# Regrouping the short TensorE work of an attention unit: transposes into slot 1, everything else into slot 4

## The chip, the cores and the metric

The kernel runs on one core of a Trainium2 chip. The metric is device time in microseconds for one execution; the median of several runs counts. A profile is one more execution, taken with the hardware profiler.

The engines are named as in the profile: PE is TensorE (PEld its weight loads), ACT is ScalarE, DVE is VectorE, POOL is GpSimd, SP is SyncE. SPq, PEq and so on are their instruction queues.

## The reference

Attention with RMS-normalized queries and keys, then a mixture of experts in which each token goes to one expert. All is float32.

```
q_n, k_n = rmsnorm(q, g_q), rmsnorm(k, g_k)          # q, k, v: (8, 12, 448, 64)
scores = q_n @ k_n^T / sqrt(64)
attn = exp(scores - max(scores)); attn /= sum(attn) + 1e-9
x = (attn @ v), heads side by side                   # 3584 tokens x 768
logits = x @ w_gate + modality_bias[modality_id]     # 8 experts
e = argmax(logits); gate = softmax(logits)[e]
out[token] = gate * (relu(x @ w1[e]) @ w2[e])        # w1: 768 x 1024, w2: 1024 x 768
```

## The kernel before

The first half of the span is attention, the second the experts; the change is in the first. Attention works in 48 **units** (u = 0 to 47), each a pair of heads of one batch row (12 heads make 6 units to a row, 8 rows). A unit has seven **slots** (j = 0 to 6); slot n = 7u + j is one turn of the loop at line 1172. In each slot TensorE first computes one tile of the transposed scores, `st` (line 848): two matmuls, four in slot 3, whose exp ScalarE writes as the tile `p`. Then it computes one tile `sa` (line 816), a rough score of the unit two ahead, of which VectorE takes the row maxima. These matmuls read operands of the type float32r. Both `st` and `sa` have two PSUM buffers.

All other TensorE work is short and is put into slots by due times:

- `tr` (line 742): four transposes of the normalized keys (g = 1) or queries (g = 0) of the unit three ahead. It returns four parts: `a0`, a ScalarE copy and two moves by DMA; `dve`, a VectorE subtraction for the low part and two more moves; `a1` and `a2`, casts on ScalarE (for queries each with a small one more).
- `mt` (line 835): transposes the seven columns of row maxima; ScalarE copies the result, and a DMA (line 843, on SyncE's queue from u = 2 on) puts it into row 64 of `ql`. There the second `st` matmul of the unit's slot 0 reads it, since the maximum is subtracted inside the matmul.
- `av` (line 887): the product of `p` with the values, four of them to a unit (c = 0 to 3), each for two heads, in plain float32: two instructions a head. After c = 3 `avcopy` takes the sum out.
- `sums` (line 904): eight matmuls every second unit, column sums of `p`. `gates` (line 913) and `recips` (line 925): once in four units. `xt` (line 946): four transposes of the output of a unit; its VectorE part writes `x`, and every third one stores it (line 967).

**What sets the order.** The dictionary `PLAN` (line 34) holds due times: `av`, `xt`, `sm`, `la`, `rc` are slots after the start of the following units for av, xt, sums, gates and recips (lines 1145 to 1170); `mt`, `tk`, `tq` are slots ahead of a unit's own start for mt and the two transposes; `first` holds single exceptions by unit. From u = 36 on, gates and recips are held to 4 and 6 at most and sums take `sml`, which is 4. Within a slot the loop writes instructions in the order of its lines, and each engine runs them in that order. `at(pre["A"], n + 1, f)` puts `f` on ScalarE ahead of the exp of the next slot, `pre["V"]` on VectorE ahead of the maximum, and `post` behind both in the slot named. The DMAs of these parts go into SyncE's queue in the same order, together with the loads of queries and keys (line 675), four loads of values (lines 666 and 668) and the x stores.

In slots of a steady unit u, the before has: slot 0 the key transposes (for u + 3), slot 1 two av (for u - 1) and mt (for u + 1), slot 2 sums and recips where due, slot 3 the query transposes, slot 4 one av and xt, slot 6 the last av and gates where due. `tr`, `mt`, `xt` and `recips` take turns on two PSUM buffers (tag "t").

Of the kernel before, what the change touches and what calls it, by code (L numbers as in the profile page):

```python
# [66 lines left out]
def kernel(  # L67
# [15 lines left out]
    V, A, G = (Deferred(e, n) for e, n in ((nc.vector, "op"), (nc.scalar, "act"), (nc.gpsimd, "dma")))  # L83
# [562 lines left out]
    if True:  # L646
# [31 lines left out]
        def sumsq(u, i):  # L678
# [156 lines left out]
        def mt(u):  # L835
            t = T[u]
            ps = ps_t.tile([128, 512], F32, tag="t", name=f"mt{u}")
            PE.transpose(ps[0:NJ, :128], t["mx"], idn)

            def act():  # L840
                ms = ms_b[u % 2]
                A.copy(ms, ps[0:NJ, :128])
                (A if u < 2 else SY).dma_start(t["ql"][64:65].rearrange("p h s -> p (h s)").bitcast(F32),
                            ms.bitcast(F32))

            return act
# [206 lines left out]
        P = PLAN  # L1053
# [6 lines left out]
        puts, done, routed = [], [], []  # L1060
# [71 lines left out]
        P = PLAN  # L1132
# [39 lines left out]
        for n in range(P["start"], NJ * NU):  # L1172
            i, j = divmod(n, NJ)
            todo = {}
            for what, *a in plan.get(n, ()):
                todo.setdefault(what, []).append(tuple(a))
            state["n"] = n
            state["rush"] = i >= P["rushat"]
            warm(P["warm"].get(n, 0))
            ex = st(i, j) if 0 <= i < NU else None  # L1180
            sm = [sa(*a) for a in todo.get("sa", ())]
            if n < 0:
                warm(P["warmn"])
            for u, c in todo.get("av", ()):
                av(u, c)
                if c == 3:
                    at(pre["A"] if j else post, n + (j > 0), lambda u=u: avcopy(u))
            for a in todo.get("sums", ()):
                sums(*a)
            for a in todo.get("gates", ()):  # L1190
                at(pre["A"], n + 1, gates(*a))
            for a in todo.get("tr", ()):
                a0, a1, a2, d_ = tr(*a)
                if a[0] < P["early"]:
                    at(pre["A"], n + 1, a1)
                    at(pre["A"], n + 1, a2)
                    at(pre["A"], n + P["late0"], a0)
                    at(pre["V"], n + P["late0"], d_)
                    continue
# [6 lines left out]
            for a in todo.get("recips", ()):
                at(pre["V"], n + 1, recips(*a))
                at(pre["V"], n + 1, lambda a=a: done.append(a[0]))
            for a in todo.get("xt", ()):
                at(pre["V"], n + 1, xt(*a))  # L1210
# [186 lines left out]
    nv = nc.values_load(state["nsl"], min_val=0, max_val=NS1 + NS2)  # L1397
# [52 lines left out]
```

## Time and profile before

| | |
|---|---|
| median of 3 runs | 1126.03 us (1123.86 to 1131.41) |
| the profiled execution | 1130.37 us, span 1128.6 us |
| TensorE busy | 1075.7 us, 95% of the span |
| VectorE, ScalarE, GpSimd busy | 858.9, 826.7, 659.0 us |
| mean granted TensorE clock | 0.978 |

In the views of the profile a row of the timeline is: start in us from the start of the span, duration, engine, line of the kernel, operation, output<-inputs by tile names, partitions x elements, and count; in brackets the time that the engine idled ahead of it and what it waited for. Tiles that share memory carry the name of the shared buffer: `w1w` holds the operands of st and sa, `xw` the high and low parts of the transposes and the copied maxima, `xrw` the normalized inputs, `at_hlw` among others the maxima, `r2w` and `at_w2lw` the exps and the values. L52 is the helper that records most ScalarE, VectorE and GpSimd work. In rows of groups the numbers after the bar are busy time, mean ns of one, and idle time ahead with its causes. Matmuls are pipelined and their ends are modelled: the difference of two starts is the safer measure.

### The profile page before, as it was taken

The numbers are of one execution on the slowest core, as the hardware profiler recorded it, in microseconds if no ns is written. First come the engines' busy times: TensorE is split into PE (matmuls) and PEld (weight loads), VectorE is DVE, ScalarE is ACT, GpSimd is POOL, SyncE is SP. The second block draws the span as 40 slices with busy tenths as digits, with TensorE's granted clock in tenths as the row PEclk, the third lists the DMA queues.
The fourth block names the chain that finished last, engine by engine and source line by source line (L and its number), as shares of the span: only waits on it lengthen the run. The fifth ranks groups of instructions, "written<-read, shape, count | busy, mean of one in ns | idle before, by whom it ended". The sixth has DMA issues, their size and how long they took to land.

```text
span 1128.6 us, 19979 instructions
## 1 busy us (share of the span) xinstructions
PE 1075.7 (95%) x6678; PEld 836.1 (74%) x6678; DVE 858.9 (76%) x1598; ACT 826.7 (73%) x1605; POOL 659.0 (58%) x665
## 2 busy tenths in 40 slices
PE   7899999999999999999999999999999999999993
PEld 6655555555455555554559899999999999999991
DVE  4577788988789788889698978767777677776770
ACT  6778888878788688876677677667876677766870
POOL 4478677779677697777864565354234433445340
PEclk8799999999999899999999999999999999999997
DMA  7656677667576777665824202111160111111360
GB/s 176 153 130 158 153 175 174 156 164 176 135 178 143 161 160 163 168 143 110 239 85 145 51 21 71 29 57 57 44 265 29 57 43 56 33 40 57 107 199 8
DMA packets 127970, 131.79 MB, mean 117 GB/s; under 512 B 68891, under 2 KB 122607, under 8 KB 126320
## 3 DMA queue, kind: packets, MB, share of 16 engines
q1 hardware_dynamic: 110212, 88.58, 33.9%
q0 software_dynamic: 17616, 41.80, 11.7%
q8 instruction: 57, 0.93, 0.4%
q14 instruction: 57, 0.47, 0.2%
q10 hardware_dynamic: 28, 0.01, 0.0%
HBM read 148.74 MB, written 22.38 MB: 152 GB/s over the span
## 4 chain that ended last, share of the span: by engine, by line
PE 74%; DVE 10%; DMA 7%; ACT 3%; issue 2%; SPq 1%; POOL 1%; ACTq 0%; DVEq 0%; POOLq 0%
PE ph L485 17%; PE py L515 16%; PE av L894 13%; PE st L855 12%; PE sa L827 4%; DMA lt<-l_d,tb_li 4%; PE tr L750 3%; DVE w1w L52 2%; DVE at_hlw L52 2%; PE xt L951 2%; DMA w1w<-xw 2%; PE sm L909 2%; PE px L468 2%; DVE xw L52 1%; DVE w2lw L52 1%
## 5 line engine op out<-in xcount | busy, mean ns | idle before, releaser
L485 PE MATMUL ph<-xw,w1w 128*128 128x256 f32 x2016 | 246.1, 283 | 3.1 <-DVE hlw L52 2.3
L485 PEld LDWEIGHTS ph<-xw,w1w 128*128 128x128 f32 x2016 | 243.9, 192 | 5.1 <-DVE hlw L52 2.5
L52 DVE TENSOR_REDUCE at_hlw<-sa 128x1 f32<-128x448 f32 x336 | 206.4, 617 | 49.5 <-PE sa L827 30.1
L52 DVE TENSOR_TENSOR w1w<-r,w1w 128x256 fp32r<-128x256 f32 x360 | 221.3, 674 | 13.3 <-ACT w1w L52 13.3
L52 ACT CAST w1w<-r 128x256 fp32r<-128x256 f32 x360 | 225.3, 726 | 0.0
L855 PE MATMUL st<-w1w 128*128 128x448 f32 (+1 forms) x480 | 177.3, 418 | 3.1 <-ACT r2w L52 3.0
L52 ACT ACTIVATE r2w<-st 128x448 f32<-128x448 f32 x168 | 91.1, 544 | 50.0 <-PE st L855 42.8
L52 ACT ACTIVATE hhw<-ph 128x512 fp32r<-128x512 f32 x56 | 33.5, 597 | 123.0 <-PE ph L485 123.0
L827 PE MATMUL sa<-w1w 128*128 128x448 f32 (+1 forms) x288 | 110.5, 384 | 9.8 <-DVE at_hlw L52 5.5
L855 PEld LDWEIGHTS st<-w1w 128*128 128x128 f32 (+1 forms) x480 | 85.7, 192 | 46.0 <-ACT r2w L52 23.7
L52 POOL TENSOR_TENSOR r2w<-r2w 128x448 f32<-128x448 f32 (+1 forms) x72 | 82.8, 1151 | 59.1 <-DVE r2w L52 18.3
L515 PE MATMUL py<-w2lw,hhw 128*128 128x384 f32 x448 | 113.9, 335 | 0.0
L52 ACT ACTIVATE at_w2lw<-st 128x448 f32<-128x448 f32 x168 | 91.0, 544 | 24.1 <-PE st L855 17.8
L855 PE MATMUL st<-w1w,w2ha 65*128 65x448 f32 x288 | 102.4, 376 | 5.3 <-DMA w1w<-xw 5.3
L52 ACT CAST w1w<-xw 64x448 fp32r<-64x448 f32 x188 | 105.3, 561 | 2.0
L52 POOL DMA_INDIRECT out_dram<-yw,lb_oi x22 | 26.7, 1215 | 123.5 <-ACT yw L52 120.5
L52 POOL TENSOR_TENSOR xrw<-r,at_hlw 112x512 f32<-112x512 f32 x95 | 97.4, 1044 | 1.0 <-PE tr L750 0.7
L515 PEld LDWEIGHTS py<-w2lw,hhw 128*128 128x128 f32 x448 | 80.8, 188 | 0.0
L52 DVE SCALAR_TENSOR_TENSOR hlw<-ph,hhw 128x512 fp32r<-128x512 f32 x56 | 38.6, 690 | 52.0 <-ACT hhw L52 51.9
L52 POOL TENSOR_TENSOR r2w<-r2w,at_w2lw 64x448 f32<-64x448 f32 (+1 forms) x48 | 55.6, 1157 | 32.3 <-DVE r2w L52 16.6
L52 ACT ACTIVATE xrw<-r 112x512 f32<-112x512 f32 (+1 forms) x124 | 64.7, 527 | 11.4 <-DMA r<-in_k_dram 8.1
L827 PEld LDWEIGHTS sa<-w1w 128*128 128x128 f32 (+1 forms) x288 | 55.6, 193 | 22.0 <-DVE at_hlw L52 9.7
(299 smaller groups left out, 2256.9 us busy)
## 6 DMA issues: line engine op xcount, KB each, us to landing
w1w<-xw SPq DMA_DIRECT2D x312, 112.0 KB
r<-in_q_dram SPq DMA_DIRECT2D x48, 224.0 KB
r<-in_k_dram SPq DMA_DIRECT2D x48, 224.0 KB
w2ha<-xw SPq DMA_DIRECT2D x72, 112.0 KB
x_d<-at_w2hb SPq DMA_DIRECT2D x8, 672.0 KB
x_d<-yw SPq DMA_DIRECT2D x8, 672.0 KB
r2w<-in_v_dram SPq DMA_DIRECT2D x48, 96.0 KB
at_w2lw<-in_v_dram SPq DMA_DIRECT2D x48, 96.0 KB
```

Source lines behind the costliest of these rows:

```text
L52: return fn(*a, **kw)
L468: PE.transpose(ps[:, i, 128 * t : 128 * t + 128], xr[t][:, 2 * g + i], idn)
L485: PE.matmul(ps[:, i], lhsT=lt_, rhs=rt_[:, c], start=n == 0, stop=n == 17)
L515: PE.matmul(ps[n][:, :384], lhsT=lt_[:, j, 128 * t : 128 * t + 128], rhs=rt_[:, 384 * n : 384 * n + 384], start=j == 0 and m == 0, stop=j ...
L750: PE.transpose(sp[:, c], src[:, c], idn[:CP, :CP])
L827: PE.matmul(ps[:, :S], lhsT=t["qq"][r, h, a : a + 128], rhs=t["kk"][h][r], start=True, stop=True)
L855: PE.matmul(ps[:, :S], lhsT=l, rhs=t["qq"][:, h] if first else t["ql"][:, h], start=first and (j != 3 or h == 0), stop=not first and (j != ...
L894: PE.matmul(t["av"][64 * h : 64 * h + 64, :S], lhsT=vv[r, u % 3, j], rhs=t["p"][r, j], start=c == 0, stop=c == 3)
L909: PE.matmul(R[g][32 * i : 32 * i + 32, :S], lhsT=sel[:, m], rhs=T[u + i // 2]["cs"][:, i % 2], start=m == 0, stop=False, tile_position=(0, ...
L951: PE.transpose(ps[:CP, 128 * c : 128 * c + 128], T[u]["xt"][:, c * CP : (c + 1) * CP], idn)
```

## The change

Two things change: numbers in `PLAN`, and the order in which the loop writes the short work of a slot. In `PLAN` (one line in the kernel, here only the entries that differ):

```diff
-'av': (1, 1, 4, 6), 'sm': 2, 'la': 6, 'rc': 9, 'mt': 6, 'tk': 21, 'tq': 18
+'av': (1, 1, 4, 4), 'sm': 4, 'la': 4, 'rc': 6, 'mt': 3, 'tk': 20, 'tq': 20
-'first': ('nq', 9): 31, ('nq', 8): 35, ('mt', 8): 50, ('mt', 5): 30, ('tk', 9): 43, ('mt', 6): 36, ('mt', 4): 22
+'first': ('nq', 9): 32, ('nq', 8): 29, ('tk', 3): 1, ('tk', 4): 8
```

In slots: key and query transposes both go to slot 1, the last av to slot 4 beside the third, mt to slot 4, sums and gates to slot 4, recips to slot 6. xt stays in slot 4 (in slots 2 and 5 for the last eight units, as before).

In the loop, `tr`, `mt`, `recips` and `xt` are now written ahead of `av`, `sums` and `gates`, and the parts of `tr` come sooner: `a0` and `dve` behind the exp and the maximum of the same slot, `a1` ahead of the next slot's exp and `a2` behind it.

```diff
             if n < 0:
                 warm(P["warmn"])
+            for a in todo.get("tr", ()):
+                a0, a1, a2, d_ = tr(*a)
+                if a[0] < P["early"]:
...
+                    continue
+                at(post, n, a0)
+                at(post, n, d_)
+                at(pre["A"], n + 1, a1)
+                at(post, n + 1, a2)
+            for a in todo.get("mt", ()):
+                at(pre["A"], n + 1, mt(*a))
+            for a in todo.get("recips", ()):
+                at(pre["V"], n + 1, recips(*a))
+                at(pre["V"], n + 1, lambda a=a: done.append(a[0]))
+            for a in todo.get("xt", ()):
+                at(pre["V"], n + 1, xt(*a))
             for u, c in todo.get("av", ()):
                 av(u, c)
...
             for a in todo.get("gates", ()):
                 at(pre["A"], n + 1, gates(*a))
-            for a in todo.get("tr", ()):
-                a0, a1, a2, d_ = tr(*a)
...
-                at(pre["A"], n + 1, a0)
-                at(pre["V"], n + 1, d_)
-                at(post, n + 1, a1)
-                at(pre["A"], n + 2, a2)
-            for a in todo.get("mt", ()):
-                at(pre["A"], n + 1, mt(*a))
...
```

The instructions themselves, their shapes and their number stay as they are.

More of the change, by code (lines that the diff above doesn't have):

```diff
@@ L33 @@
 ET = mybir.EngineType
-PLAN = {'rtj': 6, 'rushat': 36, 'av': (1, 1, 4, 6), 'xt': 4, 'xte': (2, 5), 'sm': 2, 'la': 6, 'rc': 9, 'csv': (1,), 'csj': (3, 6), 'csd': (1, 1), 'cse': (2, 1), 'sa': 14, 'mt': 6, 'tk': 21, 'tq': 18, 'nq': 26, 'nk': 26, 'sk': 49, 'sq': 50, 'rs': 48, 'ld': 58, 'first': {('sq', 0): -22, ('sk', 0): -22, ('nk', 0): -21, ('nq', 0): -20, ('sq', 1): -21, ('sk', 1): -21, ('sq', 2): -20, ('sk', 2): -20, ('nk', 1): -18, ('nq', 1): -18, ('tk', 0): -18, ('tq', 0): -18, ('sa', 0): -14, ('tk', 1): -13, ('tq', 1): -11, ('sa', 1): -7, ('mt', 0): -6, ('tk', 2): -8, ('tq', 2): -8, ('nq', 2): -14, ('nk', 2): -14, ('nq', 3): -2, ('nk', 3): -1, ('sq', 3): -8, ('sk', 3): -8, ('sq', 4): -9, ('sk', 4): -9, ('sq', 6): -6, ('sk', 6): -4, ('sk', 7): -7, ('sq', 8): 5, ('sk', 8): 5, ('nk', 7): 15, ('nq', 9): 31, ('tq', 3): 4, ('mt', 1): 0, ('nq', 5): 10, ('mt', 8): 50, ('rs', 0): -21, ('rs', 2): -18, ('nq', 8): 35, ('rs', 5): -7, ('mt', 2): 8, ('nq', 7): 18, ('mt', 5): 30, ('sk', 9): 15, ('tk', 9): 43, ('mt', 6): 36, ('nq', 6): 13, ('sa', 5): 22, ('rs', 7): 0, ('rs', 8): 6, ('mt', 4): 22, ('nk', 4): 4, ('ld', 9): 6, ('tk', 5): 15}, 'rs0': {0: 0, 2: 1, 5: 0, 7: 0, 8: 2}, 'sastep': 1, 'start': -22, 'warm': {5: 2, -6: 16, -12: 4, -7: 2, -9: 4, -21: 4}, 'warmn': 2, 'early': 1, 'late0': 1, 'pmp0': 2, 'ramp': 10, 'pmp': (0, 0, 1, 1, 1, 0, 1), 'nv': [(2, 1)], 'pmpa': (1, 0, 1, 0, 1, 1, 1), 'rush': (1, 1, 1), 'ps': [(7, 1)], 'pa': [(6, 0), (6, 1), (5, 1), (5, 0)], 'rtr': 6, 'sml': 4}
@@ new lines @@
+PLAN = {'rtj': 6, 'rushat': 36, 'av': (1, 1, 4, 4), 'xt': 4, 'xte': (2, 5), 'sm': 4, 'la': 4, 'rc': 6, 'csv': (1,), 'csj': (3, 6), 'csd': (1, 1), 'cse': (2, 1), 'sa': 14, 'mt': 3, 'tk': 20, 'tq': 20, 'nq': 26, 'nk': 26, 'sk': 49, 'sq': 50, 'rs': 48, 'ld': 58, 'first': {('sq', 0): -22, ('sk', 0): -22, ('nk', 0): -21, ('nq', 0): -20, ('sq', 1): -21, ('sk', 1): -21, ('sq', 2): -20, ('sk', 2): -20, ('nk', 1): -18, ('nq', 1): -18, ('tk', 0): -18, ('tq', 0): -18, ('sa', 0): -14, ('tk', 1): -13, ('tq', 1): -11, ('sa', 1): -7, ('mt', 0): -6, ('tk', 2): -8, ('tq', 2): -8, ('nq', 2): -14, ('nk', 2): -14, ('nq', 3): -2, ('nk', 3): -1, ('sq', 3): -8, ('sk', 3): -8, ('sq', 4): -9, ('sk', 4): -9, ('sq', 6): -6, ('sk', 6): -4, ('sk', 7): -7, ('sq', 8): 5, ('sk', 8): 5, ('nk', 7): 15, ('nq', 9): 32, ('tq', 3): 4, ('mt', 1): 0, ('nq', 5): 10, ('rs', 0): -21, ('rs', 2): -18, ('nq', 8): 29, ('rs', 5): -7, ('mt', 2): 8, ('nq', 7): 18, ('sk', 9): 15, ('nq', 6): 13, ('sa', 5): 22, ('rs', 7): 0, ('rs', 8): 6, ('nk', 4): 4, ('ld', 9): 6, ('tk', 5): 15, ('tk', 3): 1, ('tk', 4): 8}, 'rs0': {0: 0, 2: 1, 5: 0, 7: 0, 8: 2}, 'sastep': 1, 'start': -22, 'warm': {5: 2, -6: 16, -12: 4, -7: 2, -9: 4, -21: 4}, 'warmn': 2, 'early': 1, 'late0': 1, 'pmp0': 2, 'ramp': 10, 'pmp': (0, 0, 1, 1, 1, 0, 1), 'nv': [(2, 1)], 'pmpa': (1, 0, 1, 0, 1, 1, 1), 'rush': (1, 1, 1), 'ps': [(7, 1)], 'pa': [(6, 0), (6, 1), (5, 1), (5, 0)], 'rtr': 6, 'sml': 4}
@@ L1183 @@
                 warm(P["warmn"])
+            for a in todo.get("tr", ()):
+                a0, a1, a2, d_ = tr(*a)
+                if a[0] < P["early"]:
+                    at(pre["A"], n + 1, a1)
+                    at(pre["A"], n + 1, a2)
+                    at(pre["A"], n + P["late0"], a0)
+                    at(pre["V"], n + P["late0"], d_)
+                    continue
+                at(post, n, a0)
+                at(post, n, d_)
+                at(pre["A"], n + 1, a1)
+                at(post, n + 1, a2)
[6 more added lines that the diff above has]
+                at(pre["V"], n + 1, xt(*a))
             for u, c in todo.get("av", ()):
@@ L1191 @@
                 at(pre["A"], n + 1, gates(*a))
-            for a in todo.get("tr", ()):
-                a0, a1, a2, d_ = tr(*a)
[L1194 to L1199, printed above, removed]
-                at(pre["A"], n + 1, a0)
-                at(pre["V"], n + 1, d_)
-                at(post, n + 1, a1)
-                at(pre["A"], n + 2, a2)
-            for a in todo.get("mt", ()):
-                at(pre["A"], n + 1, mt(*a))
[L1206 to L1210, printed above, removed]
             if puts and n >= puts[0][0] and n - lastput[0] >= 3:
```

## The prediction

> **What bounds the kernel now.** I read the head of the page first, then TensorE's timeline through one unit, then SyncE's queue.
>
> ```profile
> span 1128.6 us, 19979 instructions
> PE 1075.7 (95%) x6678; PEld 836.1 (74%) x6678; DVE 858.9 (76%) x1598; ACT 826.7 (73%) x1605; POOL 659.0 (58%) x665
> ```
>
> TensorE is busy 95% of the time, but a busy TensorE is not TensorE at its peak, so what matters is when each matmul starts. Here is one attention unit without sums, and then the sums of the next unit (start, duration; "x4" counts instructions).
>
> ```profile
> 300.89 0.55 PE L750 MATMUL tr<-idn,xrw 112*128 112x112 f32 x4
> 301.21 0.66 PE L855 MATMUL st<-w1w 128*128 128x448 f32 x2
> 301.70 0.37 PE L827 MATMUL sa<-w1w 128*128 128x448 f32 x1
> 302.00 1.72 PE L894 MATMUL av<-r2w,at_w2lw 128*64 128x448 f32 x8
> 303.65 0.28 PE L838 MATMUL mt<-idn,at_hlw 128*7 128x128 f32 x1
> ...
> 305.21 0.37 PE L822 MATMUL sa<-xw,w2ha 128*128 128x448 f32 x1
> 305.41 0.55 PE L750 MATMUL tr<-idn,xrw 112*128 112x112 f32 x4
> ...
> 306.22 0.37 PE L827 MATMUL sa<-w1w 128*128 128x448 f32 x1
> 306.52 0.97 PE L894 MATMUL av<-r2w,at_w2lw 128*64 128x448 f32 x4
> 307.43 0.65 PE L951 MATMUL xt<-idn,at_hlw 128*112 128x128 f32 x4
> 307.83 0.66 PE L855 MATMUL st<-w1w 128*128 128x448 f32 x2
> 308.32 0.37 PE L827 MATMUL sa<-w1w 128*128 128x448 f32 x1
> 308.53 0.57 PE L855 MATMUL st<-w1w 128*128 128x448 f32 x2
> 308.94 0.37 PE L827 MATMUL sa<-w1w 128*128 128x448 f32 x1
> 309.24 0.97 PE L894 MATMUL av<-r2w,at_w2lw 64*64 64x448 f32 x4
> 310.14 0.47 PE L855 MATMUL st<-w1w 128*128 128x448 f32 x1
> ...
> 310.87 0.55 PE L750 MATMUL tr<-idn,xrw 112*128 112x112 f32 x4
> ...
> 314.15 0.36 PE L827 MATMUL sa<-w1w 128*128 128x448 f32 x1
> 314.45 0.57 PE L909 MATMUL sm<-at_w2lw,sel 128*32 128x448 f32 x2
> ...
> 315.33 0.68 PE L855 MATMUL st<-w1w 128*128 128x448 f32 x2
> ```
>
> From transpose to transpose the unit takes 310.87 - 300.89 = 9.98 us, with no idle time in any row: TensorE sets the pace here. Three things can be read off the starts. (a) Two st matmuls take 308.94 - 308.53 = 0.41 after an sa, but 0.49 after a short group (301.21 and 307.83 to the next sa): an **exit** costs 0.08. (b) From sa to the next st is 0.21 (308.32 to 308.53), from sa to av or sm 0.30 (301.70, 306.22, 314.15): an **entry** into these costs 0.09 more; into transposes none (305.21 to 305.41). (c) One value product takes 0.91 and 0.90 (306.52, 309.24 to the next row), two in a row 1.65 (302.00 to 303.65): joining two saves 0.16.
>
> The second candidate is SyncE's queue, which issues every load and every move between partitions, about 15 to a unit, in program order.
>
> ```profile
> 305.10 0.79 SPq L843 DMA_DIRECT2D w1w<-xw  x1
> 306.55 2.43 SPq L763 DMA_DIRECT2D w1w<-xw  x4
> 309.08 0.63 SPq L967 DMA_DIRECT2D x_d<-yw  x1
> ...
> 310.48 1.85 SPq L675 DMA_DIRECT2D r<-in_k_dram  x1
> ...
> 318.07 0.81 SPq L843 DMA_DIRECT2D w1w<-xw  x1
> ```
>
> ```profile
> 389.74 0.81 SPq L843 DMA_DIRECT2D w1w<-xw  x1
> ...
> 399.09 0.79 SPq L843 DMA_DIRECT2D w1w<-xw  x1
> ```
>
> ```profile
> L843 SPq DMA_DIRECT2D w1w<-xw x46: 782/792/1117, 58.5 to 567.2; - x46
> ```
>
> L843 sends a unit's row maxima and comes once a unit, so it is a clock: 45 units in 508.7 us, 11.30 us each. Without an x store the queue gets through a unit in 399.09 - 389.74 = 9.35 us. With one (every third unit) it takes 12.97, of which 306.55 - 305.10 - 0.79 = 0.66 is waiting, so 12.3; one load behind the store took 1.85. The average floor is (12.3 + 2 x 9.35) / 3 = 10.33. So TensorE binds, SyncE is less than 10% behind, and SyncE's time is uneven.
>
> **The change, part by part.** Times below are from the start of slot 1's st.
>
> *Fewer groups.* A plain unit has five short groups (slots 0, 1, 3, 4, 6), three of them with an av entry. After it there are two, each with an av. Removed: 3 exits x 0.08 = 0.24, one entry 0.095 (0.30 less 0.205), one joining 0.16 (two pairs of products where there was one pair and two singles): 0.495. How av follows transposes inside a group isn't in the trace. The nearest is sa to av, 0.095, which I keep; at the ends it is 0 or twice that, 0.095 x 2 groups x 45 = 9 us each way. Over 45 units: 0.495 x 45 = 22.3 us.
>
> *Sums, gates, reciprocal transposes.* Up to unit 36 sums had a group of their own every other unit; now they ride in slot 4: entry and exit, 0.175 x 18 = 3.1 us less. Reciprocals, which shared it, stand alone in slot 6 in one unit of four: 0.08 x 9 = 0.7 us more. From unit 36 on, the before already has them in slots 4 and 6. Gates rode with an av and still do. TensorE's average unit goes from 9.98 + 1.06/2 + 0.88/4 + 0.40/4 = 10.83 (sums 0.88 from 314.45 to 315.33, plus entry and exit 0.175, thus 1.06; gates like sums, joined; reciprocals like xt, 307.43 to 307.83) to 9.485 + 0.44 + 0.22 + 0.12 = 10.27. Sum of both parts: 22.3 + 3.1 - 0.7 = **25 us less on TensorE**.
>
> *Later transposes.* The key transpose goes from slot 0 to 1 and the query from 3 to 1, with all they issue: 8 transposes, two evacuations on ScalarE and two on VectorE right after that slot's exp and max, four casts and two small ones in slot 2, eight moves on SyncE. Behind them wait the exps and maxima of slots 2 and 3. In the long slot 1 TensorE takes 0.62 + 0.64 + 0.095 + 1.65 = 3.0, time for these engines to catch up. The first sa that needs them is six slots on. I cost this at nothing; if the cover fails, it is one operation (0.56 below) a unit, 25 us.
>
> *Reciprocals against transposes.* Both tr tiles of slot 1 now follow the reciprocals' tile in the same two buffers, one slot later; VectorE's evacuation of it stands ahead. I put half an operation there, 0.3 us (by the 0.544 row below), on 9 units: 3 us (bounds 0 and two operations, 10 us).
>
> *Row maxima: the dear one.* mt goes from slot 1 to 4, three slots later, and its DMA is queued behind all eight moves. Its row is needed by the second st matmul of the next slot 0.
>
> ```profile
> L52 ACT ACTIVATE r2w<-st 128x448 f32<-128x448 f32 x168 | 91.1, 544 | 50.0 <-PE st L855 42.8
> ...
> L52 ACT CAST w1w<-xw 64x448 fp32r<-64x448 f32 x188 | 105.3, 561 | 2.0
> ```
>
> ```profile
> 400.92 0.24 ACT L52 CAST xw<-xw 64x64 fp32r<-64x64 f32 x1
> ...
> 407.57 0.26 ACT L52 CAST xw<-mt 7x128 fp32r<-7x128 f32 x1
> ```
>
> ```profile
> 236.83 0.81 SPq L843 DMA_DIRECT2D w1w<-xw  x1
> ...
> 424.07 0.83 SPq L843 DMA_DIRECT2D w1w<-xw  x1
> ```
>
> ```profile
> 241.28 0.44 PE L855 MATMUL st<-w1w,w2ha 65*128 65x448 f32 x1 [0.66 <-DMA w1w<-xw]
> 426.41 0.47 PE L855 MATMUL st<-w1w,w2ha 65*128 65x448 f32 x1 [0.28 <-DMA w1w<-xw]
> ```
>
> ScalarE first: slot 2's st is done at 3.5 (3.0 + 0.49). Then come its exp, what is left of the casts and the exps of slots 3 and 4: 3 x 0.544 + 2 x 0.561 + 0.24 = 3.0, and the copy of the maxima, 0.26: ready at 6.75. From issue to the st that it releases, the DMA took 426.41 - 424.07 = 2.3 us, and behind a backlog 241.28 - 236.83 = 4.45. I take 2.3, since eight moves (two 2.43 rows, 4.9 us of issuing) lie between the loads and mt, in which a backlog can drain; 4.45 stays as the other end. So the row lands at 9.05. TensorE gets there by itself at 3.0 (slot 1) + 0.70 + 1.02 (slots 2, 3) + 2.85 (slot 4: 0.62 + mt and xt 0.5 + av 1.75) + 0.70 + 0.62 (slots 5, 6) + 0.2 = 9.1, and 0.88 later with sums or gates in slot 4. Slack: near 0 to 0.9, on average 0.7. The before had three slots more, and the two rows above waited even so, because SyncE's queue was late.
>
> That sets what a late queue costs. In an x-store unit SyncE needs 12.3, TensorE 10.27, the slack covers 0.7: st waits 1.33. 45 units hold 15 x stores, of which I count 13, since at the end no loads follow: **17 us given back**. Part of such waits is paid already:
>
> ```profile
> L855 PE MATMUL st<-w1w,w2ha 65*128 65x448 f32 x288 | 102.4, 376 | 5.3 <-DMA w1w<-xw 5.3
> L827 PE MATMUL sa<-w1w 128*128 128x448 f32 (+1 forms) x288 | 110.5, 384 | 9.8 <-DVE at_hlw L52 5.5 <-DMA w1w<-xw 3.1 <-DVE r2w L52 0.6
> ```
>
> 5.3 + 3.1 = 8 us, inside the 11.30. The changed due times of single units (norms of units 8 and 9, transposes and maxima of 3 to 9) move no work in or out; nothing.
>
> **Sum:** -25 + 17 - 8 + 3 = -13 us. The profiled execution took 1130.37 us (its span 1128.6), 4.3 more than the median of the runs, 1126.03. Taken off both: 1117 for an execution like the profiled one, **1113** for the median.
>
> The Trainium skill speaks against the first term. In "TensorE: Matmul & The Clock Gate", section "Step-by-step: what each phase is for", the end of one matmul overlaps the start of the next, so that back-to-back matmuls cost their columns alone; by that an order of the same matmuls is as good as any other, and the 25 would be 0. The trace disagrees: 0.41 against 0.49 for the same two st. I go by the rows, and keep the rule as a rival.
>
> **The rivals.**
>
> *TensorE alone decides.* The maxima always come in time and SyncE catches up in the units without a store, as the 9.35 row allows. Against it: 12.3 does not fit into 10.27 plus 0.7. Time: 1126 - 25 = 1101.
>
> *SyncE paces everything.* If long issues like the 1.85 fell into each unit, 9.35 + 1.2 = 10.55, the floor would be (12.3 + 2 x 10.55) / 3 = 11.1, 0.2 under now. The 9.35 row shows a unit without one. Time: 1126 - 0.2 x 45 + 3 = 1120.
>
> *Regrouping is free.* Entries and exits might belong to the instructions (weights that must load, whatever came before) and stay. Then TensorE keeps 10.83, the x-store wait is 12.3 - 10.83 - 0.7 = 0.8, 10 us on 13 units, less the 8 paid, plus 3. Time: 1131. Against: the same st costs 0.41 in one place and 0.49 in another.
>
> *The maxima's DMA takes over (slower).* The loop from slot 1 to the next slot 1 is 6.75 (maxima ready) + L (issue to landing) + 0.4 (the rest of slot 0). With L = 4.45 it is 11.6 in each unit, 12.3 with a store: (12.3 + 2 x 11.6) / 3 = 11.83, 0.53 over 11.30, 24 us on 45 units: 1150. It decides from the L at which the average is 11.30: a loop of 10.8, L = 3.65. For it speaks the 4.45 row, in a unit in which the maxima had far more lead; against it the 2.3 row. On the same side the Trainium skill ("DMA: Bandwidth & Descriptors", section "Queues, rings and completion order") says that all DMAs issued from SyncE share one ring on each DMA engine and are taken in ring order; no run here shows the rings, only that landing varies.
>
> **How the numbers follow.** Forecast 0.40, TensorE alone 0.25, SyncE paces 0.12, free 0.05, DMA takes over 0.18. A measurement here tells about 1% from no change, so the bounds are 1114.8 and 1137.3. The forecast's own range, 1104 to 1122, comes from the two ends of 9 us; it lies on the border, and I give 0.24 of its 0.40 to faster and 0.16 to within. TensorE alone: 0.25 faster. SyncE: 0.01 faster, 0.11 within. Free: 0.05 within. DMA: 0.16 slower, 0.02 within. So faster 0.50, within 1% 0.34, slower 0.16. The range: 1097 (TensorE alone, and half of the 9 us end) to 1136 (the free case with 5 us over); left out are most of the DMA case and a little below.
>
> **What would show it.** Right: in a plain unit 9.4 to 9.6 us from transpose to transpose, two exits instead of five; st waits on the DMA of w1w of 1 to 2 us in units with an x store, little in others; the interval between L843 rows 11.0 on average. Wrong: exits after av of 0.17 (the saving was no group's); waits of st on that DMA in each unit (the slower rival) or none (TensorE alone); waits of sa on VectorE or of st on ScalarE in slots 2, 3, 6 of more than 0.3 a unit (the evacuations aren't covered); waits of tr on VectorE well over 3 us in all.

## The result, and the profile after

The changed kernel takes 1165.37 us (median of 4 runs, 1159.11 to 1170.14) against 1126.65 us for the kernel before in the same session: ratio 1.0335, 95% interval 1.0302 to 1.0367. It is **slower by 3.4%**, where the prediction said 1113 us. The profiled execution took 1170.14 us.

The head of the page after:

```profile
span 1168.4 us, 19959 instructions
...
PE 1089.5 (93%) x6678; PEld 853.5 (73%) x6678; DVE 856.9 (73%) x1598; ACT 812.3 (70%) x1605; POOL 655.7 (56%) x665
```

TensorE's matmuls are the same in number (6678); its share fell and its busy time rose by 14 us. The first expert matmul (line 485) starts at 617.5 us instead of 583.2, so 34.3 of the span's 39.8 us were lost in attention. The experts' part took 550.9 us against 545.4. The kernel before with nothing but one DMA on another queue (b_actq, below) took 550.9 there too, so these 5.5 us are not put down to the change.

The steady stretch of attention is compared by windows. The columns are the length, the busy time of PE, PEld, DVE, ACT and POOL with the number of instructions, the granted clock, and the share and rate of the DMA engines. Before:

```profile
80.00:570.00 490.00, 479.72 (x2560) 274.01 (x2560) 400.81 (x800) 388.55 (x848) 374.52 (x393) 0.99 0.70 161
```

After, up to the same point of the work:

```profile
80.00:605.00 525.00, 489.65 (x2557) 288.08 (x2555) 399.25 (x796) 374.19 (x845) 372.16 (x393) 0.97 0.64 149
```

Of the 35 us, 25.1 are idle time of TensorE (490 - 479.72 = 10.3 before, 525 - 489.65 = 35.4 after) and 9.9 are busy time. Busy time times clock is 474.9 before and 475.0 after, each good to 0.005 x 490 = 2.5 us, since the clock has two digits here. With the clock followed from one microsecond of the trace to the next the products are 473 and 477. In full-clock time TensorE does **no less work than before**. Nothing of the 25 us that regrouping was to save is there.

What TensorE waited for in these stretches (total us, times, longest), after:

```profile
PE st L855 <- DMA w1w<-xw: 18.9, 13, 5.1
PE sa L827 <- DVE at_hlw L52: 9.7, 9, 2.8
PE tr L750 <- DVE lg L52: 2.7, 4, 1.1
PE tr L750 <- DVE at_hlw L52: 1.6, 2, 1.1
PE tr L750 <- POOL r2w L52: 1.3, 2, 0.8
```

and before:

```profile
PE st L855 <- DMA w1w<-xw: 3.1, 4, 1.2
PE sa L827 <- DVE at_hlw L52: 3.0, 3, 1.9
PE sa L827 <- DMA w1w<-xw: 2.9, 2, 2.2
```

Three groups have grown: the second st of slot 0, which waits for the row of maxima (15.8 us more), sa, which waits for VectorE (6.7 more), and tr (5.6 in eight waits, where there were none).

Of the 9.7 us in which sa waits for VectorE, 8.6 fall on one place in the unit: the sa of slot 4, in seven of the nine waits. It needs the buffer of slot 2's sa, so VectorE must have taken that maximum first. One such wait, on TensorE and on VectorE:

```profile
169.94 0.47 PE L827 MATMUL sa<-w1w 128*128 128x448 f32 x1 [0.80 <-DVE at_hlw L52]
```

```profile
167.54 0.61 DVE L52 TENSOR_REDUCE at_hlw<-sa 128x1 f32<-128x448 f32 x1
168.07 0.67 DVE L52 SCALAR_TENSOR_TENSOR xw<-tr,gs,xw 128x448 fp32r<-128x448 f32 x1
168.66 0.61 DVE L52 TENSOR_TENSOR xw<-tr,xw 128x448 fp32r<-128x448 f32 x1
...
169.28 0.61 DVE L52 TENSOR_REDUCE at_hlw<-sa 128x1 f32<-128x448 f32 x1
```

The two rows in the middle take the transposes of slot 1 out of PSUM, right ahead of the maximum that sa waits for. In slot 4, on the other hand, VectorE runs dry, as its group of maxima on the page shows:

```profile
L52 DVE TENSOR_REDUCE at_hlw<-sa 128x1 f32<-128x448 f32 x336 | 206.0, 618 | 131.0 <-PE sa L827 120.6
```

On the page before the same group had 49.5 us of idle time ahead of it, 30.1 of it behind sa. Counted in the trace, VectorE idles 64 us in 40 units between the sa of slot 4 and the next one (21 us before), but only 9 us in 41 units behind the sa of slot 1. So it has time where nothing waits for it, and none where the transposes have to be taken out.

The eight waits of tr stand right behind the reciprocals, in one unit of four. The name `lg`, on which half of their time falls, is written by nothing but VectorE's part of `recips`.

One unit without sums, after (TensorE's timeline; the rows between are st and sa as before):

```profile
305.19 0.93 PE L750 MATMUL tr<-idn,xrw 112*128 112x112 f32 x8
306.05 1.72 PE L894 MATMUL av<-r2w,at_w2lw 128*64 128x448 f32 x8
307.70 0.67 PE L855 MATMUL st<-w1w 128*128 128x448 f32 x2
308.21 0.36 PE L827 MATMUL sa<-w1w 128*128 128x448 f32 x1
...
310.07 0.27 PE L838 MATMUL mt<-idn,at_hlw 128*7 128x128 f32 x1
310.18 0.60 PE L951 MATMUL xt<-idn,at_hlw 128*112 128x128 f32 x4
310.71 1.87 PE L894 MATMUL av<-r2w,at_w2lw 128*64 128x448 f32 x8
312.51 0.69 PE L855 MATMUL st<-w1w 128*128 128x448 f32 x2
313.03 0.37 PE L827 MATMUL sa<-w1w 128*128 128x448 f32 x1
...
313.89 0.47 PE L855 MATMUL st<-w1w 128*128 128x448 f32 x1
...
314.40 0.36 PE L827 MATMUL sa<-w1w 128*128 128x448 f32 x1
314.60 0.45 PE L855 MATMUL st<-w1w 128*128 128x448 f32 x1
...
315.09 0.37 PE L827 MATMUL sa<-w1w 128*128 128x448 f32 x1
315.30 0.55 PE L750 MATMUL tr<-idn,xrw 112*128 112x112 f32 x4
```

Transpose to transpose it takes 10.11 us, and the shortest plain unit of the steady stretch (from mt to mt) is 10.04, where the prediction had 9.485 and the kernel before 9.97. The two groups take 2.51 + 0.10 of exit (305.19 to 307.70, then 0.51 to the sa instead of 0.41) and 2.44 + 0.11. That is 5.16 in all. The five groups of before, in the unit that the prediction shows, add up to 0.40 + 0.40 (transposes and exits), 0.095 + 1.65 + 0.03 + 0.09 (two products, mt and exit), 0.095 + 0.91 + 0.40 + 0.08 (product, xt and exit) and 0.095 + 0.90 + 0.11 (product and exit) = 5.26. So 0.10 was saved by these rows, not 0.495. And two pairs of st in the last slots take 0.51 and 0.49 to their sa instead of 0.41, which gives 0.18 back. The weight loads of these slots (PEld) say why; in brackets is the wait:

```profile
313.89 0.19 PEld L855 LDWEIGHTS st<-w1w 128*128 128x128 f32 x1 [0.25 <-ACT at_w2lw L52]
...
314.58 0.19 PEld L855 LDWEIGHTS st<-w1w 128*128 128x128 f32 x1 [0.19 <-ACT at_w2lw L52]
```

Here short slots (two st and a sa) follow each other faster than ScalarE's exps. With the short work spread over five slots, TensorE had something to do meanwhile.

The second pair of products differs from the first in one thing. Windows that open late enough show where its second product starts and what it is:

```profile
306.85 0.92 PE L894 MATMUL av<-r2w,at_w2lw 128*64 128x448 f32 x4
...
311.61 0.97 PE L894 MATMUL av<-r2w,at_w2lw 64*64 64x448 f32 x4
```

The first pair joins two products over 128 rows: 0.80 to the second product (306.05 to 306.85), then 0.85. The second pair joins one over 128 rows to one over 64: 0.90 and 0.90, as much as two single ones.

Three of the 13 waits for the row of maxima make 12.6 of the 18.9 us (3.58, 3.94 and 5.08). The first of them, on SyncE's queue, on GpSimd and on TensorE:

```profile
356.11 3.94 SPq L763 DMA_DIRECT2D w1w<-xw  x6
360.15 0.83 SPq L843 DMA_DIRECT2D w1w<-xw  x1
```

```profile
359.55 0.97 POOL L53 DMA_INDIRECT l_d<-lt,posi  x1 [0.15 <-DVE lo L53]
```

```profile
364.16 0.47 PE L855 MATMUL st<-w1w,w2ha 65*128 65x448 f32 x1 [3.58 <-DMA w1w<-xw]
```

The maxima's DMA is issued behind the unit's moves, at the moment when TensorE wants the row, and takes 364.16 - 360.15 = 4.0 us besides, right behind an indirect store of GpSimd. In ten of the 13 waits the time from issue to st is 1.9 to 2.0 us. In the three long ones it is 4.0, 5.4 and 7.3 (364.16, 426.94 and 584.87). The second has such a store 0.6 us ahead as well. The third, issued at 577.59, comes behind a load of expert weights, with the DMA engines full (a share of 1.00 or more from 573 to 581):

```profile
576.76 1.01 POOL L52 DMA_INDIRECT r<-in_moe_w_dram,ta_wi  x1 [0.15 <-issue]
```

With 2.0 us of landing the three would have waited 1.6, 0.5 and 0 us. So some 10.5 of the 18.9 us are late landing, and the other 8.4 are late issue. The lead is thin: the median from issue to the st is 2.7 us, where the kernel before had 5.1.

After the first long wait the clock falls:

```profile
364.00:367.00 3.00, 2.84 (x13) 2.36 (x13) 1.80 (x3) 2.13 (x4) 2.84 (x4) 0.70 0.88 190
```

### The profile page after: what moved, and what is told of

Same layout as the page of the kernel before. It is cut to its first block, busy times and chain, and to the rows that moved or that the text cites. A ratio compares the mean times of both kernels' runs of the same rounds, so it can differ in the third digit from the quotient of the medians.

```text
span 1168.4 us, 19959 instructions
## 1 busy us (share of the span) xinstructions
PE 1089.5 (93%) x6678; PEld 853.5 (73%) x6678; DVE 856.9 (73%) x1598; ACT 812.3 (70%) x1605; POOL 655.7 (56%) x665
## 3 DMA queue, kind: packets, MB, share of 16 engines
q0 software_dynamic: 17616, 41.80, 11.4%
## 4 chain that ended last, share of the span: by engine, by line
PE 69%; DVE 14%; DMA 8%; ACT 3%; issue 3%; POOL 2%; SPq 1%; ACTq 0%; DVEq 0%; POOLq 0%
PE ph L485 18%; PE py L515 16%; PE av L894 12%; PE st L855 10%; DVE at_hlw L52 4%; PE sa L827 4%; DMA w1w<-xw 3%; DMA lt<-l_d,tb_li 3%; DVE w1w L52 3%; PE tr L750 2%; PE px L468 2%; DVE xw L52 2%; PE sm L909 1%; PE xt L951 1%; DMA r<-in_k_dram 1%
## 5 line engine op out<-in xcount | busy, mean ns | idle before, releaser
L485 PE MATMUL ph<-xw,w1w 128*128 128x256 f32 x2016 | 248.7, 285 | 3.8 <-DVE hlw L52 2.9
L485 PEld LDWEIGHTS ph<-xw,w1w 128*128 128x128 f32 x2016 | 246.5, 194 | 5.8 <-DVE hlw L52 3.1
L855 PE MATMUL st<-w1w 128*128 128x448 f32 (+1 forms) x480 | 171.0, 404 | 4.6 <-DMA w1w<-xw 2.8
L855 PEld LDWEIGHTS st<-w1w 128*128 128x128 f32 (+1 forms) x480 | 88.1, 191 | 90.6 <-issue 20.1
L52 POOL TENSOR_TENSOR r2w<-r2w 128x448 f32<-128x448 f32 (+1 forms) x72 | 82.1, 1140 | 75.2 <-DVE r2w L52 44.7
L52 ACT ACTIVATE r2w<-st 128x448 f32<-128x448 f32 x168 | 88.5, 541 | 43.1 <-PE st L855 38.2
L52 ACT ACTIVATE at_w2lw<-st 128x448 f32<-128x448 f32 x168 | 88.5, 541 | 32.3 <-PE st L855 25.8
L52 ACT CAST w1w<-xw 64x448 fp32r<-64x448 f32 x188 | 97.4, 565 | 1.3
L855 PEld LDWEIGHTS st<-w1w,w2ha 65*128 65x128 f32 x288 | 55.5, 193 | 23.6 <-DMA w1w<-xw 19.4
```

Source lines behind the costliest of these rows:

```text
L52: return fn(*a, **kw)
L485: PE.matmul(ps[:, i], lhsT=lt_, rhs=rt_[:, c], start=n == 0, stop=n == 17)
L855: PE.matmul(ps[:, :S], lhsT=l, rhs=t["qq"][:, h] if first else t["ql"][:, h], start=first and (j != 3 or h == 0), stop=not first and (j != ...
```

## The experiments

Fourteen kernels were run. The ratio is always to the kernel before, run in the same session. Names with b_ start from the kernel before, names with a_ from the changed one.

### The place of the row of maxima

**b_mt4**: the kernel before, with the maxima alone moved to slot 4.

```diff
-'mt': 6, 'first': ('mt', 4): 22, ('mt', 5): 30, ('mt', 6): 36, ('mt', 8): 50
+'mt': 3
```

> The kernel before with one thing moved: the transpose of the row maxima goes from slot 1 to slot 4. Lead theory (the loss is the maxima's DMA having no lead; 16 us of st waits on it and a slowed clock behind the long ones): 1143 to 1152 us, with st waits on the DMA of w1w of 12 us or more. Lumps theory (the loss is VectorE and ScalarE falling behind two long slots): 1123 to 1130, st waits under 6. Recorded theory that TensorE does gain 25 us and the DMA eats it all and more: 1165 or above.

Measured: 1209.67 us, 1.0691 (1.0616 to 1.0766): dearer by itself than the whole change, and far above the 1143 to 1152. The time falls in the third range, but that range supposed a gain of 25 us on TensorE, of which the sums of 473 and 477 show nothing in the changed kernel. The st waits on the maxima are 42.5 us, spread over 28 units and not mainly in three. Here mt stands behind a product, and the query's four moves (from slot 3) are right ahead of it in SyncE's queue.

**a_mt2**: the changed kernel, maxima two slots sooner, in slot 2.

```diff
-'mt': 3
+'mt': 5
```

> The changed kernel with the transpose of the maxima in slot 2 instead of 4 (slot 1 has no free PSUM buffer for it); its DMA stays behind the eight moves. Lead theory: st waits on w1w fall under 6 us, time 1140 to 1148, since TensorE itself gained nothing and the VectorE waits stay. Lumps theory: 1158 to 1168. If TensorE had gained its 25 us: 1100 to 1125.

Measured: 1164.6 us, 1.0317 (1.023 to 1.0404), no gain that shows and not the 1140 to 1148. The st waits fell to 11.4 us in 12, not under 6, but mt itself now waited for VectorE 9.1 us in 11, for a free buffer behind the two tiles of transposes.

**a_actq**: the changed kernel, the maxima's DMA on ScalarE's queue, so that no move is ahead of it.

```diff
-                (A if u < 2 else SY).dma_start(t["ql"][64:65]...
+                A.dma_start(t["ql"][64:65]...
```

> The changed kernel with the maxima's DMA issued from ScalarE's queue for all units (the code does so for the first two), so that it waits for no other issue of SyncE. If SyncE's order is the cause: nearly all st waits on w1w go, 1140 to 1148. If the DMA lands late for another reason (traffic of the same DMA engines): the three long waits of 3.6 to 5.1 us stay, 1155 to 1162. Lumps theory: 1160 to 1170.

Measured: 1146.59 us, 1.0128 (1.0057 to 1.0198). The st waits for this DMA fell from 18.9 us to 0.2, and attention ended at 596.8 instead of 617.5. So the maxima's place in SyncE's queue costs about 2% of the 3.4%. The run does not part late issue from late landing: on ScalarE's queue the maxima are issued sooner (3.7 us ahead of the st, as median, for 2.7), and the long landings are gone as well. What is left:

```profile
PE sa L827 <- DVE at_hlw L52: 11.5, 15, 2.1
PE tr L750 <- DVE lg L52: 3.2, 5, 1.1
```

**b_mt4_actq** has both edits on the kernel before.

> The kernel before with the maxima transposed in slot 4 (as the run that took 1210) and their DMA issued from ScalarE's queue instead of SyncE's. SyncE theory (what costs is the place behind SyncE's moves and loads, not the three slots): st waits on w1w fall from 41 to under 5 us, 1125 to 1140. If three slots less are too few for the DMA itself: 1170 or above.

Measured: 1155.57 us, 1.0227 (1.0183 to 1.0272), between the two ranges given. Two thirds of the 6.9% were the queue; with nothing ahead of it the row still comes late (st waits 13.3 us in 18), so the shorter lead has a price of its own.

**b_actq**: the same queue on the kernel before, the control.

> The kernel before, unmoved, with the maxima's DMA issued from ScalarE's queue. SyncE theory: one issue in 15 less on a queue that is over 90% full, and the 6 us of DMA waits of st and sa shrink: 1112 to 1122, faster than both kernels. If TensorE alone binds: 1122 to 1130. If ScalarE's issue (0.76 us) holds up its exps: 1132 or above.

Measured: 1132.26 us, 1.0019 (0.9992 to 1.0047), in a session in which the kernel before took 1132.58, so none of the gain forecast and no loss either, though the st waits went from 3.1 us to none. In the kernel before, the maxima's place in SyncE's queue costs nothing that can be measured.

**a_mt6**: the changed kernel with the maxima back in slot 1, where they had been.

```diff
-'mt': 3
+'mt': 6, 'first': ('mt', 4): 22, ('mt', 5): 30, ('mt', 6): 36, ('mt', 8): 50
```

> The changed kernel with only the maxima back where they were (due 6 slots ahead, slot 1, with the four single exceptions of before). If the late maxima behind SyncE's moves cost about 2% and the rest is the evacuations around slot 4 (theory now): waits of st on the DMA of w1w under 5 us, ratio to before 1.008 to 1.018, as with the maxima on ScalarE's queue (1.0128). If the place of the maxima does not matter: 1.03. If the maxima's place is all there is to it: 1.00.

Measured: 1276.92 us, 1.1244 (1.1193 to 1.1296), a plain miss of the 1.008 to 1.018.

```profile
PE mt L838 <- DVE xw L52: 100.8, 41, 4.6
```

```profile
300.59 0.28 PE L838 MATMUL mt<-idn,at_hlw 128*7 128x128 f32 x1 [1.98 <-DVE xw L52]
300.80 2.76 PE L894 MATMUL av<-at_w2lw 128*64 128x448 f32 x8
```

tr, tr and mt are three tiles on two PSUM buffers: mt waits until VectorE has taken out the first, and the products stand behind it. So the moves of the parts hang together: with both transposes in slot 1, mt has no room there. The second row shows more: the pair of products takes 2.76 instead of 1.72 after only 2 us of idling. The clock in the stretch behind it:

```profile
302.00:305.00 3.00, 3.00 (x11) 1.46 (x8) 0.03 (x1) 0.30 (x1) 0.00 (x0) 0.54 0.78 175
```

### The order within a group

**a_avfirst**: the changed kernel, with the block of av, sums and gates written ahead of tr, mt, recips and xt again.

```diff
+            for u, c in todo.get("av", ()):
+                av(u, c)
...
             for a in todo.get("tr", ()):
...
-            for u, c in todo.get("av", ()):
-                av(u, c)
...
```

> The changed kernel with one thing put back in the loop: within a slot the value products, sums and gates go ahead of the transposes, as before. If transposes ahead of a product cost TensorE a drain of their own (0.86 and 0.64 us a group where the prediction counted 0.74 and 0.53), the shortest plain unit falls from 10.04 to 9.7 to 9.85. In time that is at most 10 us, and the maxima and the moves come 1.7 us later, so SyncE theory: 1165 to 1185. If order inside a slot doesn't matter: units 10.0, time within 6 us of 1165.

Measured: 1252.34 us, 1.1049 (1.1001 to 1.1096), far above both ranges. TensorE itself does not care: the slot-1 group took 2.41 + 0.09 for the entry, against 2.51. But now transposes and maxima come two products later, 1.8 us, and the row is late in nearly every unit: st waits for it 64.5 us in 44. Lead is dear: with mt at the head of slot 4 the st waits are 18.9 us, behind one product (b_mt4) 42.5, behind two 64.5, though the three kernels differ in more than that. Waits of st for exps make another 24 us.

### The products

**b_av4**: the kernel before with the products, sums, gates and reciprocals of the change.

```diff
-'av': (1, 1, 4, 6), 'sm': 2, 'la': 6, 'rc': 9
+'av': (1, 1, 4, 4), 'sm': 4, 'la': 4, 'rc': 6
```

> The kernel before with only the value products, sums, gates and reciprocals regrouped (slots 1, 1, 4, 4; 4; 4; 6). If joining the last two products saves 0.16 as the prediction has it: 0.335 us a unit and 3 us for the sums, 1108 to 1112. If the pair costs 1.80 as in the changed kernel's trace, only entry and exit go: 1115 to 1120. Lumps theory: no gain or slower, 1126 or above, with more VectorE waits of sa.

Measured: 1141.52 us (10 runs), 1.0095 (1.0061 to 1.0129). The joined pair:

```profile
307.10 1.87 PE L894 MATMUL av<-r2w,at_w2lw 128*64 128x448 f32 x8
308.90 0.65 PE L951 MATMUL xt<-idn,at_hlw 128*112 128x128 f32 x4
```

It takes 1.80, as two singles do (0.91 + 0.90): this joining saves nothing. The shortest plain unit is 9.91, 0.06 less than 9.97, so one group fewer saved no more than one exit. What has grown is waiting: sa for VectorE 9.3 us (3.0 before), sa for SyncE's moves 4.5 (2.9 before).

**b_av4_actq**, with the maxima on ScalarE's queue, asks whether SyncE's queue is behind the loss.

> The kernel before with only the value products and sums regrouped (that run took 1141.5, 1.0095 of before) and the maxima's DMA on ScalarE's queue. If its loss is SyncE's queue (4.5 us of sa waits on moves): ratio 1.000 to 1.005. If VectorE's (9.3 us of sa waits): 1.007 to 1.012. If TensorE had gained 0.335 us a unit under it: 0.985 to 0.995.

Measured: 1151.64 us, 1.017 (1.0108 to 1.0231), above all three ranges. It got no better, and the waits of sa for VectorE stayed (9.0 us). So the maxima on SyncE's queue are not behind it; that the waits for VectorE are is not shown by itself.

### The transposes

**b_tr1**: the kernel before with both transposes in slot 1.

```diff
-'tk': 21, 'tq': 18, 'first': ('tk', 9): 43, ('nq', 8): 35, ('nq', 9): 31
+'tk': 20, 'tq': 20, 'first': ('tk', 3): 1, ('tk', 4): 8, ('nq', 8): 29, ('nq', 9): 32
```

> The kernel before with only the transposes moved: key and query transposes both in slot 1 (behind two value products, ahead of the maxima's transpose); loop order, products and the maxima's slot stay. Theory now (a change of kind inside a group costs TensorE what an exit does): the shortest unit stays at 9.9 to 10.05 us and the ratio to before lies between 0.995 and 1.012, the upper half if VectorE's and ScalarE's evacuations of eight transposes at once hold up sa. The prediction's step (two exits of 0.08 fall away, evacuations hidden): 9.82 and 0.993. Rival, that the eight moves in one row on SyncE's queue are by themselves dear: 1.02 or more, with waits of st on the DMA of w1w over 12 us.

Measured: 1191.07 us, 1.0513 (1.0472 to 1.0555), a miss again, and for the same reason as a_mt6:

```profile
PE mt L838 <- DVE xw L52: 45.5, 39, 3.9
```

The buffers swamp the run: these waits and one more of mt make 47 of its 58 us.

**b_tr1_mt4_actq** takes buffers and queue out of the way: both transposes in slot 1, maxima in slot 4 on ScalarE's queue, products and loop order as before.

> The kernel before with both transposes in slot 1 and the maxima in slot 4 on ScalarE's queue, that is, what is left when the third tile no longer waits for a buffer in slot 1 (48.7 us in 42 waits in the run that moved the transposes alone) and SyncE's moves no longer lie ahead of the maxima. Products, sums, gates and the loop's order stay as before. If a change of kind inside a group costs what an exit does: shortest unit 9.9 to 10.05, ratio 1.000 to 1.012, waits of mt on VectorE near 0. If the moved transposes save the prediction's two exits: 9.82 and 0.993 or less. If their evacuations are what the changed kernel still lacks with the maxima on ScalarE's queue (1.0128): 1.013 or more, with sa waiting for VectorE 8 us or more.

Measured: 1155.81 us, 1.0184 (1.014 to 1.0227), the third of its cases. The shortest unit is 10.10, the next ones 10.29, where two exits less should have made 9.82.

```profile
122.74 0.99 PE L750 MATMUL tr<-idn,xrw 112*128 112x112 f32 x8
123.49 0.65 PE L855 MATMUL st<-w1w 128*128 128x448 f32 x2
...
125.21 0.63 PE L855 MATMUL st<-w1w 128*128 128x448 f32 x2
125.85 0.47 PE L827 MATMUL sa<-w1w 128*128 128x448 f32 x1
```

```profile
125.85 0.19 PEld L827 LDWEIGHTS sa<-w1w 128*128 128x128 f32 x1 [0.40 <-DVE at_hlw L52]
```

Eight transposes behind av take 0.75, where two groups of four cost 2 x (0.32 + 0.08) = 0.80 with their exits. In slot 4 the step from st to sa is 0.64 (125.21 to 125.85) instead of 0.41, and the weight load shows that sa waits for a maximum of VectorE, which has the evacuations of eight transposes ahead of it. In all, sa waits for VectorE 10.6 us in 15, and 8.3 of it at the sa of slot 4, as in the changed kernel. b_mt4_actq, which differs from this kernel in the place of the transposes alone (and of two norms that go with them), has 1.2 us of such waits: **the moved transposes bring them.** The time shows it less plainly, since st still waits 5.3 us for the maxima, which follow a product here, and 13.3 in b_mt4_actq.

### What is left

**a_actq_sq** is a_actq with the squares of the norms and their loads a few slots sooner.

```diff
-'sk': 49, 'sq': 50, 'ld': 58
+'sk': 53, 'sq': 52, 'ld': 62
```

> The changed kernel with the maxima's DMA on ScalarE's queue (that run took 1146.6), and the squares of the norms moved to the ends of slots 3 and 4 (loads four slots earlier), so that VectorE's two reductions of 0.67 us fall into the long slot 4, in which it idles 2.8 us. Lumps theory (the remaining 15 us are VectorE idle in slot 4 and behind elsewhere): sa waits on VectorE fall from 11.5 to under 6 us, 1133 to 1141. If the rest is TensorE's own time, or SyncE: 1144 to 1150, or slower through late loads.

Measured: 1186.74 us, 1.0459 (1.0382 to 1.0536), a miss. The waits of sa for VectorE did fall, from 11.5 to 4.7 us, and were more than given back by waits of st: 12.0 us on the moves and maxima, 9.6 on loads and 4.1 on exps.

**a_mt3_actq**: a_actq with the maxima in slot 3, as a group of their own ('mt': 4).

> The changed kernel with the maxima one slot sooner (slot 3, a group of its own) and on ScalarE's queue: slot 4 has one tile less for ScalarE and VectorE, the row has one slot more. If the rest of 1.3% of the changed kernel on that queue is the crowd in slot 4: ratio 1.005 to 1.012 though one group more; if it is TensorE's order and the evacuations of the products and transposes: 1.012 to 1.02, the shortest unit 10.1 (one exit more).

Measured: 1143.85 us, 1.0092 (1.0058 to 1.0127), in the first range given; but a_actq's interval covers it, so that slot 4's crowd is the rest is not shown. TensorE shows something else:

```profile
132.77 0.27 PE L838 MATMUL mt<-idn,at_hlw 128*7 128x128 f32 x1
132.80 0.45 PE L855 MATMUL st<-w1w 128*128 128x448 f32 x1
133.09 0.37 PE L855 MATMUL st<-w1w,w2ha 65*128 65x448 f32 x1
```

The lone mt takes 0.03 to the st and makes this st 0.29 long instead of 0.205, 0.11 in all, just what it took inside the group of slot 4 (310.07 to 310.18). The shortest unit is 10.03 with three groups, 10.04 with two. One group more costs nothing here.

**a_put** tries the long waits behind GpSimd's indirect stores: the changed kernel with these stores held to slot 1 up to unit 36.

```diff
-            if puts and n >= puts[0][0] and n - lastput[0] >= 3:
+            if puts and n >= puts[0][0] and n - lastput[0] >= 3 and (j == 1 or i >= 36):
```

> The changed kernel with GpSimd's scatter of routing entries issued only in slot 1 of a unit (up to unit 36), away from the maxima's DMA. If the long st waits (3.6, 3.9 us) come from that scatter on the same DMA engines: they go, and with them the slowed clock behind them, 1150 to 1158. If from SyncE's own traffic: they stay, 1160 to 1170.

Measured: 1163.62 us, 1.0275 (1.0234 to 1.0316). Up to unit 36 no wait for the maxima is longer than 1.36 us, so the long ones there did come with the stores. The third, behind the load of weights, stays (4.3 us). But sa waits for VectorE rose to 15.5 us, TensorE's waits in the steady stretch are 34.9 us in all against 34.7, and the time is not told apart from 1.0335. What was won at one wait came back at another.

No version beats the kernel before; b_actq equals it.

## Why the prediction was wrong, point by point

**Fewer groups, 22.3 us: the step that failed.** Three exits of 0.08 were taken as removed with their groups, and one entry of 0.095 as the price of a product behind transposes. The runs show that TensorE pays where one kind of matmul follows another, inside a group as at its end. Eight transposes take 0.86 to the product behind them, where two times four took 0.32 each to the st: 0.86 - 0.64 = 0.22 more, and not 0.095. The exits behind products are 0.10 and 0.11, in the kernel before too (310.14 to the sa at 310.66 is 0.52), neither 0.08 nor the 0.17 named as a sign. A lone mt costs 0.11 ahead of xt (310.07 to 310.18) as it does ahead of st with its exit (a_mt3_actq). "Joining two saves 0.16" was read from the first pair of a unit and applied to the second, which takes 1.80 joined and saves nothing. So the groups gave 0.10 of the 0.495 a unit, and st waiting for exps in the short slots took that back (0.18 in the unit shown). Together the plain unit is 10.04 for 9.97, and TensorE's work 477 us for 473. The 9 us that the prediction allowed at either end covered only how av follows transposes, and 0.22 lies beyond twice 0.095.

That was the rival "regrouping is free", given 0.05. Its sentence from the Trainium skill ("TensorE: Matmul & The Clock Gate", section "Step-by-step: what each phase is for": back-to-back matmuls cost their columns alone) agrees with the two sums of 473 and 477 us to 1%, though not with single rows, where a change of kind does cost. The prediction set one such row, 0.41 against 0.49, against the rule; the row was right, and what it was worth to the sum was wrong. The rival's time, 1131, was too low for the reasons that follow.

**Sums, gates, reciprocals, 3 us less on TensorE:** nothing of it is left in the sums.

**Later transposes, "costed at nothing": failed.** The cover was to be the long slot 1. In the unit shown VectorE takes the maximum of slot 1's sa (164.10 on TensorE) only at 167.54, since it still has other work, and the evacuations follow in slots 2 and 3. The sa of slot 4 then waits: 6.7 us more of such waits in all, and the pair b_mt4_actq and b_tr1_mt4_actq (1.2 and 10.6 us) shows that the transposes bring them. The prediction named the price, "one operation a unit, 25 us", and a sign, more than 0.3 us a unit in slots 2, 3 and 6; 9.7 us in 45 units is 0.22, and it came in slot 4. b_av4 has waits of sa for VectorE of this size without the transposes, at other places of the unit.

**Reciprocals against transposes, 3 us:** the right mechanism, and 5.6 us, inside its bounds of 0 and 10: all eight waits of tr follow the reciprocals.

**Row maxima, +17 - 8 = +9: the right place, too small, and the 17 near by luck.** Idle time on the moves and maxima went from 3.1 + 2.9 = 6.0 to 18.9 + 0.3 = 19.2. The slack of 0.7 was right (a lead of 2.7 and a landing of 2.0). But the prediction had 1.33 in each x-store unit from a late queue. Nine of the 13 waits do stand in such units, eight of them with 0.3 to 0.9; 12.6 us came in three waits, and 10.5 of that from late landing, which the prediction had only as its other end, 4.45, and in the slower rival. With a_actq the place in the queue is worth (1.0335 - 1.0128) x 1126 = 23 us, more than the waits themselves; a lower clock behind long waits is part of that, the rest was not traced. The L843 rows are (604.6 - 59.1) / 45 = 12.12 us apart, where 11.0 was forecast.

**The slower rival** (1150, given 0.18) had the right side and the right queue. Its mechanism, a landing time of 4.45 in every unit, did not come: long landings are three, though they made over half of these waits. **SyncE paces everything** has b_actq against it: one issue in 15 less on that queue, and 1.0019. **TensorE alone** fell with the first term.

The terms as measured, in the steady stretch: TensorE's work +4 instead of -25; its lower clock +6; maxima and moves +13 instead of +9; sa on VectorE +7 instead of nothing; tr behind the reciprocals +6 instead of +3; the rest -1: 35 us. Of these the clock is not a cause of its own: in the stretch shown it falls right behind a long wait.

**What stays open.** Once the maxima are out of SyncE's queue, 0.9 to 1.3% remain. They go with waits for VectorE of some 15 us in a_actq (sa 11.5, tr 3.2), and b_av4 shows 0.95% with the products alone; but the one attempt to take those waits away (a_actq_sq) lost more elsewhere, so this share was argued and not shown. How the 2% of the queue divide between late issue and late landing was not tested. Nor was the reason why the second pair of products gains nothing by joining: the trace shows that it changes from 128 rows to 64 in the middle, and no run changes that alone.

## What to carry to other kernels

A price read from one pair of rows (an exit, a joining) belongs to that neighbourhood; before it is multiplied by all units, look for a second place in the trace where the same edge stands between other neighbours. Short work between long chains is also what fills the gaps in which slower engines catch up: bundling it saved TensorE nothing here, and left VectorE idle in one slot and late in another. When a transfer is moved later, count what is queued ahead of it at its new place, and when tiles are moved into one slot, count their buffers: two dear experiments, 5% and 12%, had three tiles on two buffers.

## What the runs showed of the hardware

- Where one kind of matmul follows another, TensorE's step is longer, inside a run of short work or at its end: 0.08 to 0.11 us at st behind short work, 0.09 at a product behind sa, 0.22 at a product behind eight transposes (0.86 for 2 x 0.32), 0.10 at a product over 64 rows behind one over 128 (0.90 for 0.80). At transposes behind sa it is nothing (305.21 to 305.41 before).
- After 2.8 and 2.0 us without a matmul the granted clock fell to 0.55 and 0.54 in the stretches behind (a_mt6), for some 3 us; after 2.2 us in the next unit it did not. The Trainium skill ("TensorE: Matmul & The Clock Gate", section "HAM oscillation — how this bites in real kernels") gives gaps of over about 3.4 us as what throttles the clock. The measurement decides: shorter gaps can do it.
- The maxima's DMA lets st go 1.9 to 2.0 us after its issue in ten of the changed kernel's 13 waits (302.08 to 304.08 is one). It took 4.0 and 5.4 us with an indirect store of GpSimd issued 0.6 us ahead of it, and 3.4 in the kernel before (491.48 to 494.89) at the same distance. With the store only 0.1 us ahead it took 1.9 (220.41 to 222.34).
